# A two-layer decode step with finer pieces: K turned in halves or later, V of seven pairs in 2 KB pieces with one copy of P, new tables

## The chip, the cores and the metric

The kernel runs on one core of one Trainium2 chip. The metric is the device time of one execution in microseconds. The core's engines work beside each other and wait for one another on semaphores: TensorE (PE, with its weight loads shown as PEld), VectorE (DVE), ScalarE (ACT), GpSimd (POOL), and SyncE (SP), which here only issues transfers. Each engine takes its own instructions in the order in which they were written.

## The reference

Two layers, each an attention over a cache and a gated product, for 4 sequences with one new token each (bf16 in and out):

```python
# B=4, D=512, 32 query heads, 8 K/V heads, cache of 4096 keys, head size 128, F=1792
def _A_ref(x, k_cache, v_cache, wq, wo):
    q = (x @ wq) in heads;  k, v = caches, each head used by 4 query heads
    p = _softmax(einsum("bhqd,bhkd->bhqk", q, k) * (128 ** -0.5))
    return einsum("bhqk,bhkd->bhqd", p, v) in rows @ wo
def _B_ref(x, w_gate, w_up, w_down):
    return (_sigmoid(x @ w_gate) * (x @ w_up)) @ w_down

x = A_x
x = x + _A_ref(_layernorm(x), A_k_cache, A_v_cache, A_wq, A_wo)
x = x + _B_ref(_layernorm(x), B_w_gate, B_w_up, B_w_down)
x = x + _A_ref(_layernorm(x), A_k_cache, A_v_cache, A_wq, A_wo)   # same caches and weights
x = x + _B_ref(_layernorm(x), B_w_gate, B_w_up, B_w_down)
```

One K or one V of one K/V head and one sequence is 4096 x 128 in bf16, 1 MB. There are 64 of them, and both layers read all of them.

## The kernel before

**Pairs and steps.** The work is cut into 32 pairs: a layer, a sequence and two K/V heads, in the order of the table `ORDER`. The main loop (L1754) has 33 steps. Step k computes scores and softmax of pair k and the product with V (PV) of pair k-1; its parts stand in a fixed order with nine numbered places (0 to 8) between them, and tables say which further work stands at which place.

**Slots and loads.** K and V lie in 12 slots of 1 MB. 31 of the 64 tiles, named in `RET`, stay in SBUF from layer 1 to layer 2; the others are loaded twice. SP issues the loads in the order of the string `LOADS`, and `pump()` issues the next one as soon as a slot is free; a slot becomes free when the scores (`scores`, L1163) have read a K, or PV (L1365) a V. So the place of a score or PV group on PE sets when a load goes out. Loads have 8 KB per partition in one piece; the two V of the last pair come in four parts with 2 KB each (`v_parts`). The 4 MB of wq become four more slots when the last q product has read them, in step 27; the loads left then, 8 MB, are the last ones.

**One step of attention.** DVE turns K in place with a 32x32 stream transpose (`k_turn`, L1148), whole or as two halves. `first_turn` turns the first K of the next pair at one of three places, and the second K follows before place 4. The table `STEP` holds those choices and whether the first PV stands before the score products (`pv_first`). PE multiplies K with a spread q (L1163), DVE takes maxima (L1200 to L1206), PE spreads them over the partitions (L1223), DVE reduces again (L1236), ACT computes the exponential (L1248) with its sum, POOL adds sums (L1262), PE turns the result (`ptrans`, L1293) into the PSUM tile `PT`. From there 16 pieces of 32x64 are copied to `pT`, by ACT (L1319) and DVE (L1313); `SHARE` gives for each pair how many quarters DVE takes (0: all 16 on ACT, 1: 12 and 4, 2: 8 and 8). PV of one head is 32 matmuls in four groups, each waiting for its quarter of P; `PV_WIDE` repeats the four columns of P up to that width. After normalising (L1456) comes the product with wo (`wo_mm`, L1509, or in row form with a turn, L1487 to L1500, where `WO_ROW` says so), and `wo_add` (L1530) adds it to x. The last pair writes its exponential in the order in which the keys lie in the turned rows, with a stride of four, and its P is copied in two halves (L1300, L1301).

**The pass between the layers.** For each sequence, when its last pair of layer 1 is done, a pass of 23 parts runs: layer norm sums (L742 and L804), up and gate products (L963), gating, turning of the row (L1006), down product (L1077, L1099), layer norm, q product (L1024), its scaling and turning (L1038 to L1055), spreading of q (L868 to L893). `PLACES` gives each part's step and place. `FILL` adds matmuls with no use (L1182) at some places. After the last step come the output's layer norm and gated product (L1889 to L1945) and the store of 4x512 values.

## Time and profile before

| | us |
|---|---|
| median of 3 runs | 304.77 (304.65 to 306.59) |
| profiled execution, own time | 305.46 |
| its span, first to last instruction | 303.7 |
| mean granted clock of TensorE | 0.864 |
| PE / PEld busy | 227.6 / 158.5 |
| DVE / ACT / POOL busy | 206.3 / 130.7 / 26.2 |
| loads | 116.35 MB, mean 383 GB/s |

The profile is of one execution. Busy time of an engine is the time in which it carries out an instruction; waiting and issuing are not in it. A row of a group reads: line, engine, operation, written and read tiles, shapes, count, busy us and mean ns of one, and the engine's idle time just ahead of it with what ended that. A row of the timeline has the start in us from the span's start, the duration, and "x" with the number of instructions that were put together. The clock is a share of TensorE's full speed.

### The profile page before, as it was taken

What the parts mean: (1) busy time and instruction counts of PE and PEld (TensorE: products, weight loads), DVE (VectorE), ACT (ScalarE), POOL (GpSimd) and SP (SyncE); (2) the same over time, 40 slices, a digit from 0 to 9 for tenths busy, and PEclk for the clock granted to TensorE, in tenths of its full rate; (3) what the DMA queues carried; (4) which work ended last, traced back from release to release, by engine and by line L of the source; (5) the groups of instructions that cost most, each with busy time, mean ns of one, the idle gap of its engine ahead of it and who ended that gap; (6) DMA issues with size and microseconds to landing.
All of it is one profiled execution on the core that took longest, in us unless ns stands there. A gap on an engine that the chain in (4) does not pass through costs nothing.

```text
span 303.7 us, 11574 instructions
## 1 busy us (share of the span) xinstructions
PE 227.6 (75%) x5043; PEld 158.5 (52%) x5043; DVE 206.3 (68%) x611; ACT 130.7 (43%) x522; POOL 26.2 (9%) x108
## 2 busy tenths in 40 slices
PE   0355268589668888686996878788868988987896
PEld 0331024456544565465564656655445865665685
DVE  4727577877639359666952798884689467779834
ACT  1012074654505247344371676614566472547420
POOL 0000000000000010000000100000101100012200
PEclk9999999778857998996697777958875997999799
DMA  7999999999999989999999999999999998999910
GB/s 289 422 406 401 417 415 421 419 419 421 418 418 398 396 327 381 421 423 420 413 401 410 420 422 412 419 418 396 377 407 423 401 409 309 364 404 423 395 70 3
DMA packets 19166, 116.35 MB, mean 383 GB/s; under 512 B 1960, under 2 KB 1964, under 8 KB 6444
## 3 DMA queue, kind: packets, MB, share of 16 engines
q1 hardware_dynamic: 19116, 115.62, 94.0%
q8 instruction: 39, 0.64, 0.8%
q14 instruction: 11, 0.09, 0.1%
HBM read 115.61 MB, written 0.00 MB: 381 GB/s over the span
## 4 chain that ended last, share of the span: by engine, by line
PE 37%; DMA 35%; DVE 14%; SPq 6%; ACT 4%; issue 2%; POOL 0%; DVEq 0%
DMA slot<-in_A_v_cache_dram 24%; PE O_ps L1365 11%; PE S_ps L1163 7%; DMA wd<-in_B_w_down_dram 6%; DVE slot L1148 6%; DMA wo<-in_A_wo_dram 5%; PE M_ps L1024 3%; SPq L521 3%; ACT pT L1319 3%; PE O_ps L1509 3%; PE MS L1182 2%; SPq L540 2%; DVE pT L1313 1%; DVE small L1200 1%; PE M_ps L963 1%
## 5 line engine op out<-in xcount | busy, mean ns | idle before, releaser
L1319 ACT ACTIVATE pT<-PT 32x64 bf16<-32x64 f32 x396 | 84.9, 214 | 35.2 <-PE PT L1293 30.3
L1148 DVE STREAM_TRANSPOSE slot<-slot 128x1024 f32<-128x1024 f32 (+1 forms) x59 | 94.4, 1605 | 4.8 <-DMA slot<-in_A_k_cache_dram 4.7
L1365 PE MATMUL O_ps<-pT,slot 128*128 128x32 bf16 (+4 forms) x1952 | 66.9, 188 | 14.7 <-DMA slot<-in_A_v_cache_dram 8.5
L1365 PEld LDWEIGHTS O_ps<-pT,slot 128*128 128x128 bf16 x1952 | 60.8, 98 | 24.3 <-DMA slot<-in_A_v_cache_dram 9.4
L1163 PE MATMUL S_ps<-slot,qz 128*32 128x256 bf16 x976 | 47.7, 333 | 8.4 <-DVE slot L1148 5.0
L1248 ACT ACTIVATE pe<-S_ps,small 128x256 bf16<-128x256 f32 x32 | 15.5, 484 | 52.5 <-DVE small L1236 52.4
L1163 PEld LDWEIGHTS S_ps<-slot,qz 128*32 128x32 bf16 x976 | 25.6, 110 | 21.4 <-DVE slot L1148 6.9
L1262 POOL TENSOR_TENSOR small<-small 128x1 f32<-128x1 f32 x64 | 12.3, 193 | 221.2 <-ACT pe L1248 218.7
L1313 DVE CAST pT<-PT 32x64 bf16<-32x64 f32 x100 | 22.0, 220 | 3.7 <-PE PT L1293 2.2
L1509 PE MATMUL O_ps<-oT,wo 128*128 128x32 bf16 x640 | 21.3, 186 | 3.2 <-ACT wo L636 1.7
L636 ACT ACTIVATE wo<-M_ps 128x512 bf16<-128x512 f32 x14 | 8.3, 595 | 34.3 <-PE M_ps L626 34.2
L1509 PEld LDWEIGHTS O_ps<-oT,wo 128*128 128x128 bf16 x640 | 19.4, 99 | 4.9 <-DVE oT L1456 2.3
L626 PE MATMUL M_ps<-wo,row 64*128 64x512 bf16 x56 | 12.2, 524 | 8.0 <-DMA wo<-in_A_wo_dram 5.2
L1456 DVE TENSOR_TENSOR oT<-O_ps,rden 128x8 bf16<-128x8 f32 x31 | 5.0, 161 | 19.1 <-PE O_ps L1365 15.5
L641 DVE CAST wo<-M_ps 128x512 bf16<-128x512 f32 x14 | 9.5, 680 | 12.0 <-PE M_ps L626 11.8
L1200 DVE TENSOR_REDUCE small<-S_ps 128x1 f32<-128x256 f32 x32 | 13.2, 412 | 5.8 <-PE S_ps L1163 5.6
L1182 PE MATMUL MS<-ident_bf 128*128 128x256 bf16 x79 | 15.1, 332 | 2.4 <-DVE rden L1281 2.0
L893 POOL TENSOR_TENSOR qz<-qc,norm 128x128 bf16<-128x128 bf16 x32 | 12.6, 399 | 42.2 <-ACT qc L879 42.0
L1223 PE MATMUL MS<-row_max,mask_f 128*128 128x16 bf16 x64 | 6.7, 177 | 10.3 <-DVE row_max L1206 10.1
L1223 PEld LDWEIGHTS MS<-row_max,mask_f 128*128 128x128 bf16 x64 | 4.2, 105 | 17.5 <-DVE row_max L1206 14.8
L1293 PE MATMUL PT<-ident_bf,pe 128*128 128x128 bf16 x64 | 10.0, 244 | 3.7 <-ACT pe L1248 3.5
L1182 PEld LDWEIGHTS MS<-ident_bf 128*128 128x128 bf16 x79 | 7.8, 114 | 5.7 <-DVE rden L1281 2.2
(142 smaller groups left out, 230.6 us busy)
## 6 DMA issues: line engine op xcount, KB each, us to landing
slot<-in_A_v_cache_dram SPq DMA_DIRECT2D x51, 1024.0 KB, 9.9
slot<-in_A_k_cache_dram SPq DMA_DIRECT2D x40, 1024.0 KB, 10.0
wq<-in_A_wq_dram SPq DMA_DIRECT2D x4, 1024.0 KB, 7.6
wo<-in_A_wo_dram SPq DMA_DIRECT2D x8, 512.0 KB, 16.5
wq<-in_A_k_cache_dram SPq DMA_DIRECT2D x3, 1024.0 KB, 10.0
slot<-in_A_v_cache_dram SPq DMA_DIRECT2D x8, 256.0 KB, 16.6
wg<-in_B_w_gate_dram SPq DMA_DIRECT2D x2, 896.0 KB, 15.3
wu<-in_B_w_up_dram SPq DMA_DIRECT2D x2, 896.0 KB, 11.2
```

Source lines behind the costliest of these rows:

```text
L626: (lambda h, i, rows: lambda e: e.matmul(ps[h][:, :], lhsT=spread_w[i][rows, :], rhs=wo_sb[rows, c + i, :], start=(i == 0), stop=(i == 1), ...
L893: lambda e: e.tensor_tensor(qz_sb[z][:, :, 0:4 * REP].rearrange("p i (a r) -> p i a r", r=REP), qc_sb[:, b, u:u + 2, :, :].rearrange("p u ...
L1148: dve(lambda e: e.transpose(kf, kf), writes=[f"s{st}"])
L1163: (lambda t, b2, e_, w0, s: lambda e: e.matmul(S_ps[p][32 * s:32 * s + 8 * REP, 0:2 * P], lhsT=qzf[:, w0:w0 + 8 * REP], rhs=ktv[:, :, s, : ...
L1182: lambda e: e.matmul(MS[:, 2 * P:4 * P].rearrange("p (i m) -> p i m", i=2), lhsT=ident_bf[:, :], rhs=wide_id, start=True, stop=True,)
L1200: lambda e: e.tensor_reduce(m, S_ps[p][:, 0:2 * P], AX.X, ALU.max),
L1248: lambda e: e.activation(to, frm, ACTF.Exp, bias=nm_sb[p], scale=exp_scale, accum_out=sm_sb[p][0],),
L1262: (lambda n: lambda e: e.tensor_tensor(sm_sb[p][n + 1], sm_sb[p][n], top(sm_sb[p][n]), ALU.subtract))(n),
L1313: (lambda dst, frm: lambda e: e.tensor_copy(dst, frm))(dst, frm),
L1319: (lambda dst, frm: lambda e: e.activation(dst, frm, ACTF.Copy))(dst, frm),
L1365: (lambda x, c, j: lambda e: e.matmul(O_ps[p][:, ul * OW:ul * OW + PV_WIDE[g]].rearrange("p (w n) -> p w n", n=REP), lhsT=vv[:, x * JG + c ...
L1509: (lambda c, r: lambda e: e.matmul(wide_out(O_ps[p], OWO + c, nb), lhsT=wo_sb[:, u * REP + r, bass.ds(2 * P * (c // 2) + c % 2, P, step=2) ...
```

## The change

Eight things change.

1. The first K of a pair may be turned in halves, the second half one place later; the second K may be turned at one of three places (before place 4 as before, after place 5, or after place 7 at the end of the step). `STEP` holds both choices (`cut`, `late`).
2. Seven pairs get `SHARE` 6 (pairs 6, 12, 24, 27) or 7 (pairs 5, 19, 28). Their V are loaded in 2 KB pieces, in the order of four quarters of the keys (12 loads; the two V of pair 28 stay from pair 24), their exponential is read with a stride from PSUM and written plainly, and P is then one 128x256 copy, by ACT (6) or DVE (7). PV of a head is one group of 32 matmuls that waits for that copy.
3. The last exponential also reads with the stride and writes plainly.
4. With `WO_ROW` 2, the turn behind the row form of wo and the addition to x are put off to the next place or wo product (`undone`, `finish`).
5. `LAST` offers other orders for the last step; the table's value picks 0, the order of before.
6. `ORDER` and `RET` are new: sequence 3 of layer 2 ends with heads 2 and 3 rather than 6 and 7, and of that last pair only one V comes in four parts. 31 tiles are still kept.
7. `PLACES`, `FIRST_AT`, `LOADS`, `WO_AT`, `WO_ORDER`, `WO_TURN`, `WSUM`, `AHEAD` are new.
8. `SHARE`, `PV_WIDE` and `FILL` are new also for the other pairs: small copies of P on ACT from 396 to 320, on DVE from 100 to 64.

In the core of the diff, the tables are written in one line each, those of order and retention are left out:

```diff
-SHARE = (0, 1, 0, 2, 0, 1, 2, 0, 0, 2, 2, 1, 1, 1, 0, 0, 0, 0, 1, 1, 1, 0, 0, 2, 0, 1, 1, 2, 1, 1, 1)
+SHARE = (2, 2, 0, 0, 1, 7, 6, 0, 1, 1, 0, 0, 6, 2, 0, 0, 0, 0, 1, 7, 1, 0, 0, 1, 6, 1, 1, 6, 7, 0, 2)
-STEP = (6, 6, 6, 9, 5, 22, 12, 19, 6, 21, 16, 22, 9, 10, 23, 12, 9, 9, 9, 21, 21, 15, 19, 18, 21, 12, 15, 4, 3, 8, 0, 7, 8)
+STEP = (59, 9, 16, 35, 65, 37, 14, 24, 24, 9, 71, 6, 4, 59, 70, 12, 18, 30, 18, 40, 58, 9, 18, 12, 2, 11, 27, 10, 53, 25, 69, 48, 18)
-PV_WIDE = (32, 32, 32, 96, 32, 64, 48, 32, 48, 64, 32, 32, 48, 48, 32, 48, 32, 32, 32, 48, 64, 32, 32, 128, 48, 64, 48, 48, 64, 32, 96, 48)
+PV_WIDE = (32, 48, 64, 64, 32, 32, 32, 64, 48, 48, 32, 32, 48, 32, 96, 32, 64, 48, 64, 48, 32, 32, 64, 96, 64, 64, 48, 64, 96, 64, 64, 64)
-WO_ROW: 1 for pairs 7, 8, 14, 20, 27, 28, 31
+WO_ROW: 2 for pairs 7, 8, 12, 14, 15, 28; 1 for pairs 11, 19, 20, 22, 26, 27, 29
 PLACES, batch 3 (step counted from the batch's first, place in the step):
-        (1, 8), (1, 8), (1, 8), (1, 8), (2, 0), (2, 0),
-        (2, 1), (2, 1), (2, 2), (2, 2), (2, 4), (2, 6),
-        (2, 6), (2, 7), (2, 7), (2, 7), (2, 7), (2, 7),
-        (2, 7), (3, 0), (3, 0), (3, 4), (3, 6),
+        (1, 8), (2, 0), (2, 0), (2, 1), (2, 2), (2, 2),
+        (2, 2), (2, 2), (2, 2), (2, 3), (2, 3), (2, 6),
+        (2, 6), (2, 8), (2, 8), (2, 8), (2, 8), (2, 8),
+        (2, 8), (3, 0), (3, 0), (3, 2), (3, 2),
-FILL: 79 matmuls in 18 places
+FILL: 90 matmuls in 25 places
...
@@ -500,6 +502,13 @@
     def take():
         return free.pop(0)
 
+    def by_quarters(n):
+        return n < NU - 2 and SHARE[n // 2] > 5
+
+    for b in range(Bn):
+        for u in RET[b]["v"]:
+            assert by_quarters(pos[0, b, u]) == by_quarters(pos[1, b, u])
+
     def v_parts(s, n):
         _, b, u = seq[n]
         rows = A_v_cache[b, u].rearrange("(a p j) d -> a p (j d)", a=4, p=P)
@@ -535,6 +544,9 @@
                     continue
                 src = A_v_cache[b, u].rearrange("(p j) d -> p (j d)", p=P)
             dst = slot[s][:, :]
+            if kind == "v" and by_quarters(n):
+                dst = dst.rearrange("p (a m) -> p a m", a=4)
+                src = A_v_cache[b, u].rearrange("(a p j) d -> p a (j d)", a=4, p=P)
             S.dma(
                 "sp",
                 (lambda dst, src: lambda e: e.dma_start(dst, src))(dst, src),
@@ -1134,6 +1146,8 @@
             lambda: q_spread(b0, 1),
         ]
 
+    half_turned = set()
+
     def k_turn(i, part=None):
         if i >= NU or not loaded("k", i):
             return
@@ -1143,6 +1157,10 @@
         st = where["kt", b, u]
         kf = slot[st][:, :].bitcast(dt.float32)
         half = NJ * DH // 4
+        if part == 0:
+            half_turned.add(i)
+        else:
+            half_turned.discard(i)
         if part is not None:
             kf = kf[:, part * half:(part + 1) * half]
         dve(lambda e: e.transpose(kf, kf), writes=[f"s{st}"])
@@ -1151,6 +1169,7 @@
         l, b, _ = seq[2 * g]
         p = g % 2
         i = 2 * g + ul
+        assert i not in half_turned
         st = where["kt", b, seq[i][2]]
         ktv = slot[st].rearrange("p (x s j t k e) -> p x s j t k e", x=XJ, s=4, j=2, t=2, e=2)
         qzf = qz_sb[p].rearrange("p i w -> p (i w)")
@@ -1241,9 +1260,9 @@
             writes=["rmw", f"nm{p}"],
         )
         to, frm = pe_sb[p].rearrange("p j m -> p (j m)"), S_ps[p][:, 0:2 * P]
-        if g == NP - 1:
-            to = pe_sb[p].rearrange("p j (k x) -> p j x k", x=XJ)
-            frm = frm.rearrange("p (j x k) -> p j x k", j=2, x=XJ)
+        if g == NP - 1 or SHARE[g] > 5:
+            to = pe_sb[p].rearrange("p j (k x) -> p j k x", x=XJ)
+            frm = frm.rearrange("p (j x k) -> p j k x", j=2, x=XJ)
         act(
             lambda e: e.activation(
                 to,
@@ -1301,6 +1320,14 @@
             dve(lambda e: e.tensor_copy(pT_last[64:P, :], PT[64:P, 0:2 * P]), reads=["PT"], writes=["q1"])
             return
         pT = pT_sb[p]
+        if SHARE[g] > 5:
+            to = pT.rearrange("p x n j h -> p (x n j h)")
+            keys = [f"pT_{x}{a}" for x in range(XJ) for a in ("", "_0", "_1", "_2")]
+            if SHARE[g] == 6:
+                act(lambda e: e.activation(to, PT[:, 0:2 * P], ACTF.Copy), reads=["PT"], writes=keys)
+            else:
+                dve(lambda e: e.tensor_copy(to, PT[:, 0:2 * P]), reads=["PT"], writes=keys)
+            return
         src = PT[:, 0:256].rearrange("p (n a h) -> p n a h", n=16, h=REP)
         for x in range(XJ):
             for a in range(4):
@@ -1328,6 +1355,30 @@
         s = where["v", b, u]
         pT = pT_sb[p]
         vv = slot[s].rearrange("p (j d) -> p j d", d=DH)
+        if by_quarters(i):
+            assert PV_WIDE[g] >= 2
+            pq = pT.rearrange("p x n j h -> p (x n j h)").rearrange("p (j n a h) -> p j n a h", j=2, a=4, h=REP)
+            vq = slot[s].rearrange("p (a s j d) -> p a s j d", a=4, s=4, j=2)
+            fns = []
+            for a in range(4):
+                for sj in range(8):
+                    fns.append(
+                        (lambda a, c, j: lambda e: e.matmul(
+                            O_ps[p][:, ul * OW:ul * OW + PV_WIDE[g]].rearrange("p (w n) -> p w n", n=REP),
+                            lhsT=vq[:, a, c, j, :],
+                            rhs=pq[:, j, 4 * ul + c, a, :].unsqueeze(1).broadcast_to([P, PV_WIDE[g] // REP, REP]),
+                            start=(a == 0 and c == 0 and j == 0),
+                            stop=(a == 3 and c == 3 and j == 1),
+                        ))(a, sj // 2, sj % 2)
+                    )
+            rd = [f"s{s}"] + [f"pT_{x}{a}" for x in range(XJ) for a in ("", "_0", "_1", "_2")]
+            if ul == 0:
+                S.group("pe", fns, reads=rd, writes=[f"O{p}"])
+            else:
+                S.last_write[f"O{p}"] = S.group("pe", fns, reads=rd)
+            if l == 1 or not kept("v", i):
+                free.append(where.pop(("v", b, u)))
+            return
         if PV_WIDE[g] < 2:
             many = 2 - PV_WIDE[g]
             for x in range(XJ):
@@ -1494,14 +1545,22 @@
                     )
             S.group("pe", fns, reads=rd, writes=[f"O{p}"])
             act(lambda e: e.activation(row_f, rows, ACTF.Copy), reads=[f"O{p}"], writes=["row0"])
-            fns = []
+            turns = []
             for i in range(2):
-                fns.append(
+                turns.append(
                     (lambda i: lambda e: e.matmul(
                         turned[:, :, i, 0:nb], lhsT=row_f[:, i:2 * P:2], rhs=sel_f[:, :, 0:nb], start=True, stop=True
                     ))(i)
                 )
-            S.group("pe", fns, reads=["row0", "sel"], writes=[f"O{p}"])
+
+            def turn():
+                S.group("pe", turns, reads=["row0", "sel"], writes=[f"O{p}"])
+                wo_add(g, p)
+
+            if WO_ROW[g] == 2:
+                undone.append(turn)
+            else:
+                turn()
             return
         for c in range(KD):
             for r in range(2 * REP):
@@ -1532,9 +1591,16 @@
             writes=[f"x{b0}", f"x{b1}"],
         )
 
+    undone = []
+
+    def finish():
+        while undone:
+            undone.pop()()
+
     def wo_pair(g, p):
         wo_mm(g, p)
-        wo_add(g, p)
+        if not WO_ROW[g]:
+            wo_add(g, p)
 
     ln_a(0, Bn)
     ln_b(Bn)
@@ -1599,6 +1665,7 @@
     assert max(WSUM) < (NP - 3, 8)
 
     def do_steps(g, w):
+        finish()
         if FILL.get((g, w)):
             fill(FILL[g, w])
         for m in wo_steps.pop((g, w), ()):
@@ -1672,6 +1739,7 @@
         )
 
     assert NP % 2 == 0
+    LAST = (0, 1, 2, 4, 5, 6)[STEP[NP] % 6]
     XS, XM = S_ps[0], M_ps[0][:, 0:1]
 
     def x_others():
@@ -1741,6 +1809,7 @@
 
     def do_wo(gs, p):
         for g in gs:
+            finish()
             waiting.remove(g)
             wo_pair(g, p)
 
@@ -1784,11 +1853,20 @@
         if nxt is not None and fresh.get(seq[2 * nxt][:2]) != k:
             q_blocks(nxt)
         do_steps(k, 0)
-        turn_at, pv_first, halves = STEP[k] % 3, STEP[k] // 3 % 2, STEP[k] // 6
+        turn_at, pv_first, cut, late = STEP[k] % 3, STEP[k] // 3 % 2, STEP[k] // 6 % 4, STEP[k] // 24
+        halves = cut % 2 == 1 and sg is not None and nxt is not None
 
         def first_turn(at):
             if nxt is not None and turn_at == at:
-                k_turn(2 * nxt)
+                k_turn(2 * nxt, 0 if cut > 1 else None)
+                pump()
+            elif nxt is not None and cut > 1 and turn_at + 1 == at:
+                k_turn(2 * nxt, 1)
+                pump()
+
+        def second_turn(at):
+            if nxt is not None and late == at:
+                k_turn(2 * nxt + 1, 1 if halves else None)
                 pump()
 
         first_turn(0)
@@ -1804,7 +1882,6 @@
                     do_wo(wo_ready(k + 1)[:1], (k + 1) % 2)
 
         wo_at(0)
-        halves = halves and sg is not None and nxt is not None
         if pv_first and vg is not None and sg is not None:
             pv(2 * vg)
             pump()
@@ -1820,16 +1897,16 @@
         wo_at(1)
         first_turn(2)
         do_steps(k, 3)
-        if nxt is not None:
-            k_turn(2 * nxt + 1, 1 if halves else None)
-            pump()
+        first_turn(3)
+        second_turn(0)
         do_steps(k, 4)
         if vg is not None and not pv_first and sg is not None:
             pv(2 * vg)
             pump()
         wo_at(2)
         do_steps(k, 5)
-        if sg == NP - 1:
+        second_turn(1)
+        if sg == NP - 1 and LAST & 3 == 0:
             ptrans(sg)
         if vg is not None:
             if sg is not None:
@@ -1837,15 +1914,25 @@
                 pump()
                 normalise(vg)
                 normed[seq[2 * vg]] = k
+                if sg == NP - 1 and LAST & 3 == 1:
+                    ptrans(sg)
             else:
+                if LAST & 3 == 2:
+                    ptrans(vg)
+                if LAST & 4:
+                    do_wo([g for g in wo_ready(k) if g != vg], (vg + 1) % 2)
+                    finish()
+                    x_others()
                 pv_last(vg, 0, 0, 4)
                 normalise_last(0)
                 waiting.remove(vg)
                 assert len(waiting) <= 1
-                do_wo(wo_ready(k), (vg + 1) % 2)
+                if not LAST & 4:
+                    do_wo(wo_ready(k), (vg + 1) % 2)
+                    finish()
+                    x_others()
                 assert not waiting
                 others_done()
-                x_others()
                 mean_old()
                 pv_last(vg, 1, 0, 2)
                 mean_old_mm()
@@ -1862,6 +1949,7 @@
             ptrans(sg)
         wo_at(3)
         do_steps(k, 7)
+        second_turn(2)
         if vg is not None and sg is not None and vg in ends:
             close(vg, k)
         if k == NP - 3:
```

## The prediction

> **What bounds the kernel now.** I read the page first (busy shares, slices, queues, chain), then a table of 4 us windows, then the groups by shape, and last the timeline of three places that the windows point to.

> ```profile
> span 303.7 us, 11574 instructions
> PE 227.6 (75%) x5043; PEld 158.5 (52%) x5043; DVE 206.3 (68%) x611; ACT 130.7 (43%) x522; POOL 26.2 (9%) x108
> q1 hardware_dynamic: 19116, 115.62, 94.0%
> PE 37%; DMA 35%; DVE 14%; SPq 6%; ACT 4%; issue 2%; POOL 0%; DVEq 0%
> ```

> The load queue is busy for 94.0% of the span, more than any engine, yet the chain that ends last is only 35% transfers: no resource is full all the time. Where the stream breaks is in the windows (columns: PE, PEld, DVE, ACT, POOL busy us, granted clock, DMA share, GB/s).

> ```profile
> core 0: us, PE busy (x) PEld busy (x) DVE busy (x) ACT busy (x) POOL busy (x), PEclk, DMA share, GB/s
> 104.00:108.00 4.00, 3.02 (x64) 1.68 (x64) 1.71 (x7) 0.69 (x1) 0.00 (x0) 1.00 1.03 367
> 108.00:112.00 4.00, 3.83 (x109) 3.09 (x109) 3.03 (x16) 2.61 (x12) 0.76 (x2) 1.00 0.75 268
> 112.00:116.00 4.00, 3.34 (x100) 2.40 (x88) 2.01 (x3) 2.32 (x11) 0.74 (x3) 1.00 1.00 373
> 216.00:220.00 4.00, 2.95 (x86) 2.19 (x86) 3.31 (x7) 2.76 (x13) 0.76 (x2) 1.00 0.94 350
> 244.00:248.00 4.00, 3.02 (x97) 2.44 (x94) 3.25 (x9) 2.75 (x11) 0.74 (x3) 1.00 1.02 420
> 252.00:256.00 4.00, 4.00 (x67) 1.90 (x59) 3.72 (x9) 0.71 (x2) 0.00 (x0) 0.59 0.69 233
> 256.00:260.00 4.00, 3.64 (x101) 2.78 (x94) 2.91 (x7) 1.24 (x4) 0.16 (x1) 1.00 0.99 391
> 260.00:264.00 4.00, 3.67 (x77) 2.81 (x77) 2.90 (x16) 2.31 (x12) 0.23 (x2) 1.00 0.98 344
> 264.00:268.00 4.00, 3.22 (x97) 2.21 (x86) 2.33 (x12) 1.12 (x4) 0.00 (x0) 1.00 0.93 363
> 284.00:288.00 4.00, 3.74 (x98) 2.58 (x95) 3.21 (x10) 1.88 (x9) 1.99 (x8) 0.75 1.04 385
> ```

> The undisturbed rate is 420 GB/s; 115.62 MB at that rate take 275 us. The three windows from 104 fall short of it by 53, 152 and 47 GB/s, together 252 x 4 us / 420 = 2.4 us of lost transfer; 252 to 268 loses 3.3 us in the same way, 216:220 another 0.7. Behind the last window shown the stream ends, and what follows is a tail of computing. Gains can come from these places and from the tail. Elsewhere the stream runs, and shorter work only waits for it.

> **Row copies of P (seven pairs).** Each pair copies P to the PV matmuls' layout in 16 pieces.

> ```profile
> L1319 ACT ACTIVATE pT<-PT 32x64 bf16<-32x64 f32 x396 | 84.9, 214 | 35.2 <-PE PT L1293 30.3
> L1313 DVE CAST pT<-PT 32x64 bf16<-32x64 f32 x100 | 22.0, 220 | 3.7 <-PE PT L1293 2.2
> L1248 ACT ACTIVATE pe<-S_ps,small 128x256 bf16<-128x256 f32 x32 | 15.5, 484 | 52.5 <-DVE small L1236 52.4
> L879 ACT ACTIVATE qc<-M_ps 128x128 bf16<-128x128 f32 x8 | 1.9, 280 | 9.2 <-PE M_ps L868 9.1
> L1898 ACT ACTIVATE slot<-PT 128x128 f32<-128x128 f32 x1 | 0.3, 278 | 6.6 <-PE PT L1889 6.6
> DMA slot<-in_A_v_cache_dram 24%; PE O_ps L1365 11%; PE S_ps L1163 7%; DMA wd<-in_B_w_down_dram 6%; DVE slot L1148 6%; DMA wo<-in_A_wo_dram 5%; PE M_ps L1024 3%; SPq L521 3%; ACT pT L1319 3%; PE O_ps L1509 3%; PE MS L1182 2%; SPq L540 2%; DVE pT L1313 1%; DVE small L1200 1%; PE M_ps L963 1%
> ```

> The tables take the pieces from 396 to 320 on ACT and from 100 to 64 on DVE: 76 x 0.214 + 36 x 0.220 = 24.2 us. Seven whole 128x256 copies come instead. No row has that copy; it lies between 0.280 (L879, half as many columns) and 0.484 us (as many, with the exponential), and I take 0.45, near the second, so 3.2 us. Net 21.0 of 106.9 us, 19.6%. The chain holds 3% + 1% of 303.7 us of these copies, 12.1 us, of which some 4.5 lie in the tail (the 2.73 quoted there and eight DVE pieces), costed below: 7.6 x 0.196 = **-1.5 us**. Bounds: 0, if the stream was the next limit wherever they stood, and -3.0, if it was nowhere and pairs on the chain were hit twice as often. PV now waits for all of P and not for its first quarter, but all is there in 0.45 us, where the first ACT quarter took 4 x 0.214.

> The exponential of these pairs reads PSUM with a stride. For the kind, L879 (strided read, 280 ns) against L1898 (plain, 278 ns) says that it costs nothing; bound 7 x 0.36 us = +2.5, were it as dear as the strided write of the last exponential (0.83 us below, against (15.5 - 0.83) / 31 = 0.47 for the others).

> **V in 2 KB pieces.** Twelve loads change from 8 KB to 2 KB pieces and one V less comes as separate quarters. The rows for 2 KB are the last V's quarters: 385 GB/s at a share of 1.04 in 284:288, against 420. That is 1.05 MB at 2.72 for 2.50 us, +0.2 each, 12 x 0.2 - 0.2 = +2.2 us if each stands on a full stream. Some fall beside the gaps of steps 6 and 26, and stretches of the chain are not transfers at all (65%): I take **+0.8**, between 0 and +2.2. [...]

> **Step 26, the deepest gap.** Here the order of batch 3's pass and of the loads is told by the timeline.

> ```profile
> 243.69 0.33 SPq L540 DMA_DIRECT2D slot<-in_A_v_cache_dram  x1
> 245.43 0.33 SPq L540 DMA_DIRECT2D slot<-in_A_k_cache_dram  x1
> 249.99 0.39 PE L742 MATMUL M_ps<-xT,small 128*128 128x4 f32 x2
> 251.75 0.81 PE L963 MATMUL M_ps<-wu,xc_bf 128*1 128x448 bf16 x8 [0.26 <-DVE norm L815]
> 252.33 1.07 PE L1163 MATMUL S_ps<-slot,qz 128*32 128x256 bf16 x16
> 253.44 11.88 SPq L540 DMA_DIRECT2D slot<-in_A_v_cache_dram  x5
> 256.12 1.14 PE L1365 MATMUL O_ps<-pT,slot 128*128 128x64 bf16 x32
> 265.69 0.80 SPq L540 DMA_DIRECT2D wq<-in_A_k_cache_dram  x2
> ...
> slot<-in_A_v_cache_dram SPq DMA_DIRECT2D x51, 1024.0 KB, 9.9
> ```

> From 245.43 to 253.44 no load is issued: the next V waits for a slot that only the scores at 252.33 free, and those stand on PE behind the layer norm (L742, L804) and the first wu product. Queued data runs out and 252:256 moves 233 GB/s. The new places put these scores straight behind L742, so they can run at 250.4 and the V goes out at about 251.4, 2.0 us sooner. The first PV of that step, at 256.12 before, moves ahead of the second wu half and of wg with four fills; it frees its V about 2 us sooner, but sets the gate path back by 1.14 + some 0.6 less the 1.07 of the scores that left: +0.7. That PV also waits for the V issued at 243.69; by the median of 9.9 us to landing (last row, from the page) it is there at 253.6, where PE would now arrive at 252.6 or so: up to 1.0 more, with wu, wg and pair 27's scores queued behind it. At the end of that path the q product releases wq (265.69), and 8 MB of loads wait for it. So between -2.2 (the gap's 3.3 us mostly filled) and +1.7; I take **-0.9**, as the V that starts sooner is certain from the order on PE and the landing is not.

> **Step 20.** 216:220 is short because a K waits there for a PV that stands behind two q row products.

> ```profile
> 212.55 2.03 PE L1024 MATMUL M_ps<-wq,xc_bf 128*1 128x512 bf16 x16
> 214.63 0.96 PE L1365 MATMUL O_ps<-pT,slot 128*128 128x48 bf16 x32
> 215.62 0.33 SPq L540 DMA_DIRECT2D slot<-in_A_k_cache_dram  x1
> ```

> The PV now precedes the last product (half of 2.03): the K goes 1.0 us sooner, against 0.7 us of loss: **-0.5** (0 to -0.7). The like edit in step 6 puts the first PV ahead of a q half but adds four fills there; both are about a microsecond: 0 (-0.9 to +0.5).

> **Tail.** The last pair's scores end with the stream, and from then on each step follows the one before.

> ```profile
> 286.00 2.73 ACT L1319 ACTIVATE pT<-PT 32x64 bf16<-32x64 f32 x12 [2.27 <-PE PT L1293]
> 288.24 0.08 DVE L1236 DVE_READ_ACCUMULATOR2_ANT small<- 128x1 f32 x1
> 288.76 0.83 ACT L1248 ACTIVATE pe<-S_ps,small 128x256 bf16<-128x256 f32 x1
> 289.77 1.55 PE L1365 MATMUL O_ps<-pT,slot 128*128 128x96 bf16 x32
> ```

> The exponential's maximum is there at 288.32, but ACT is in the twelve copies of pair 30 until 288.73: with eight (DVE takes the other four, off this path) it starts 0.4 sooner. Its write is now contiguous, 0.83 to 0.47: -0.36. PV of pair 30 goes from 96 to 64 columns wide; the 64-wide one above takes 1.14, so -0.4 for the one that stands between the exponential and the last pair's PV. Sum **-1.2** (-1.9 with both PVs; 0 if the last K, now turned in halves about the softmax of pair 30, comes later by as much).

> **Edits at nothing.**

> ```profile
> L1182 PE MATMUL MS<-ident_bf 128*128 128x256 bf16 x79 | 15.1, 332 | 2.4 <-DVE rden L1281 2.0
> L1148 DVE STREAM_TRANSPOSE slot<-slot 128x1024 f32<-128x1024 f32 x38 | 46.4, 1220 | 2.6 <-DMA slot<-in_A_k_cache_dram 2.5
> ```

> 38 to 42 half turns and whole turns 21 to 20, 11 more fills, wider PVs up to 96 columns, put-off row turns and `wo` row forms: DVE (68%) and PE have the room while transfers run; without that cover the fills would be 11 x 15.1 / 79 = +2.1 us, the four half turns less one whole (two halves), 2 x 1.22 = +2.4. Retained K and V change places only; the megabytes stay.

> **Sum.** -1.5 + 0.8 - 0.9 - 0.5 - 1.2 = **-3.3 us**. The profiled execution took 305.46 us (span 303.7 and 1.76 around it) and would come to 302.2; the median of the runs is 0.69 lower, 304.77, and comes to **301.5**. A measurement of this kernel can tell some 1% from no change: 301.7 to 307.8 is "the same".

> **Rivals.** *Gaps close (298.7).* With the copies' relief at -3.0 and step 26 at -2.2, the rest as above: -6.1. For: two loads of step 26 move by 2 us, into a gap of 3.3, and pairs 6, 24 and 27 beside the gaps are among the seven. Against: a load goes out only when its own slot is free, so a gap closed in one step can open in the next.

> *Nothing upstream arrives (305.3).* The stream keeps its length, 2 KB costs its +2.2 (or the strided read its +2.5), and only the tail's -1.2 and step 20's -0.5 remain: +0.5 (+0.8). For: 94.0% queue share. That the change does not do what it says is this case too: copies that were hidden anyway.

> *K turned too late (308.3).* In eight steps the second K is now turned behind the copies and the step's last small products, right ahead of the next step.

> ```profile
>   DVE slot L1148: 11.9, 11
> ```

> That row (PE's idle time ahead of scores, us and times, by what ended it) says that 11 turns already keep PE waiting 11.9 us, 1.08 each. PE takes its work in order, so PV, `wo` and the pass behind those scores wait, and with them every slot that they free. Eight more such waits are 8.6 us; the chain's share outside transfers and their queue is 55%, so +4.7, less the tail's 1.2: +3.5. It decides from the point where a late turn ends after PE's other work of the next step's first half. Against: in most steps the first K's scores and a PV (about 1 us each) stand ahead of the second K's.

> **How the numbers follow.** Forecast 0.36 (own range 299.8 to 303.3), gaps close 0.24, nothing arrives 0.20, late turns 0.20. Faster by over 1%: 0.24 and somewhat over half of the forecast's, less what the gap case leaves above 301.7: 0.44. Slower by over 1%: 0.20 and a little of the third case, 0.22. Within 1%: 0.34. The range, 297.5 to 308.5, takes in the gap case and most of the late turns.

> **What would show it.** Right: the 252:256 window above 330 GB/s and the V of step 26 issued within 7 us of the load before; wq's K within 264 to 266 or sooner; last exponential 0.47 us; whole copies 0.38 to 0.48; windows with 2 KB pieces near 385 to 400 GB/s. Wrong: PE's idle time on K turns well over 11.9 us, whole copies near 0.8, or a gap of the stream that has only moved to another step.

## Result and profile after: 1.1% slower, and the profiled loss lies behind the release of wq

The changed kernel took 310.3 us (median; 307.8 to 311.1), 1.0114 times the kernel before beside it, with a 95% interval of 1.0066 to 1.0161. Run once more as a control on another chip it took 1.0057 (1.0012 to 1.0102). The forecast was 1.1% faster. Ratios compare undisturbed runs of both kernels (the profile of `block_shifted` is of a disturbed one, so no time is read from it), and only ratios of one chip are held against each other closely, since the kernel before itself had medians of 305.7 to 307.4 us over the chips.

The page of the changed kernel, with the lines that answer to those of before:

```profile
span 309.1 us, 11450 instructions
PE 227.0 (73%) x5030; PEld 160.6 (52%) x5030; DVE 201.2 (65%) x581; ACT 116.7 (38%) x452; POOL 26.2 (8%) x108
q1 hardware_dynamic: 23292, 115.62, 92.9%
PE 37%; DMA 30%; DVE 17%; SPq 8%; ACT 4%; issue 3%; POOL 0%; DVEq 0%; ACTq 0%
```

ACT is 14 us less busy and DVE 5 us, near the 21.0 us in all that the copies' arithmetic gave, and transfers hold less of the chain (30% for 35%). The span is 5.4 us longer. The windows show where these are not lost (columns as before):

```profile
96.00:100.00 4.00, 3.28 (x65) 2.32 (x65) 1.99 (x8) 0.37 (x1) 0.00 (x0) 1.00 1.05 387
108.00:112.00 4.00, 2.32 (x65) 1.53 (x66) 1.23 (x7) 0.66 (x2) 0.76 (x2) 0.94 0.93 337
216.00:220.00 4.00, 2.77 (x83) 2.27 (x81) 2.56 (x9) 0.07 (x1) 0.00 (x0) 0.83 1.02 424
252.00:256.00 4.00, 3.83 (x82) 2.21 (x78) 3.77 (x9) 1.15 (x2) 0.00 (x0) 1.00 0.94 348
260.00:264.00 4.00, 3.45 (x35) 1.40 (x39) 2.68 (x15) 3.09 (x13) 0.00 (x0) 0.72 0.97 356
264.00:268.00 4.00, 3.79 (x103) 2.72 (x95) 1.68 (x6) 0.18 (x1) 0.00 (x0) 0.86 0.49 151
288.00:292.00 4.00, 4.00 (x85) 2.88 (x88) 2.77 (x14) 2.27 (x10) 2.18 (x8) 0.63 0.49 182
```

The gaps that the prediction named have shrunk: 268 to 337 GB/s at 108, 350 to 424 at 216, 233 to 348 at 252. Summed over all 4 us windows, the stream leads before's by 0.78 MB at 264 us, 1.86 us at 420 GB/s. In the window behind it falls to 151 GB/s (363 before) and the whole lead is gone. From there both streams run alike and end in the same window (182 and 176 GB/s at 288). The 5.4 us come after that point, on PE; in the chain that ended last, no transfer stands behind 262 us, neither before nor after the change:

```profile
265.75 1.70 SPq L552 DMA_DIRECT2D wq<-in_A_k_cache_dram  x3
...
270.77 0.89 PE L1366 MATMUL O_ps<-pT,slot 128*128 128x64 bf16 x25
273.11 0.38 PE L1366 MATMUL O_ps<-pT,slot 128*128 128x64 bf16 x7 [1.45 <-issue]
279.04 4.35 PE L1366 MATMUL O_ps<-pT,slot 128*128 128x96 bf16 x64
283.54 3.64 ACT L1346 ACTIVATE pT<-PT 32x64 bf16<-32x64 f32 x16 [2.11 <-PE PT L1312]
294.12 0.47 ACT L1267 ACTIVATE pe<-S_ps,small 128x256 bf16<-128x256 f32 x1 [1.07 <-DVE small L1255]
294.86 1.12 PE L1416 MATMUL O_ps<-pT,slot 128*128 128x64 bf16 x32
```

wq is released at 265.75 us, as before (265.69). The last exponential starts at 294.12 (288.76 before), and what follows takes 15 us in both, of which more below. Between the maxima of pairs 28 and 29 pass 6.8 us (3.7 before), of pairs 30 and 31 6.9 (5.2), and 2.5 us (1.8) to the last exponential. In these rows stand a stop of PE of 1.45 us in the middle of one PV with nothing named that it waits for, a PV of pair 28 of 4.35 us for 64 matmuls, and sixteen copies of pair 29.

### The profile page after: what moved, and what is told of

Its sections match the earlier page's. It is cut to its first block, busy times and chain, and to the rows that moved or that the text cites. A ratio compares the mean times of both kernels' runs of the same rounds, so it can differ in the third digit from the quotient of the medians.

```text
span 309.1 us, 11450 instructions
## 1 busy us (share of the span) xinstructions
PE 227.0 (73%) x5030; PEld 160.6 (52%) x5030; DVE 201.2 (65%) x581; ACT 116.7 (38%) x452; POOL 26.2 (8%) x108
## 3 DMA queue, kind: packets, MB, share of 16 engines
q1 hardware_dynamic: 23292, 115.62, 92.9%
## 4 chain that ended last, share of the span: by engine, by line
PE 37%; DMA 30%; DVE 17%; SPq 8%; ACT 4%; issue 3%; POOL 0%; DVEq 0%; ACTq 0%
DMA slot<-in_A_v_cache_dram 16%; DMA slot<-in_A_k_cache_dram 8%; DVE slot L1166 8%; PE O_ps L1416 7%; DMA wo<-in_A_wo_dram 6%; PE S_ps L1182 5%; PE O_ps L1366 5%; SPq L552 5%; ACT pT L1346 3%; SPq L530 2%; PE M_ps L1036 2%; PE O_ps L1568 2%; PE M_ps L975 2%; PE MS L1201 2%; DVE pT L1340 1%
## 5 line engine op out<-in xcount | busy, mean ns | idle before, releaser
L1166 DVE STREAM_TRANSPOSE slot<-slot 128x1024 f32<-128x1024 f32 (+1 forms) x62 | 96.8, 1568 | 3.5 <-DMA slot<-in_A_k_cache_dram 3.4
L1346 ACT ACTIVATE pT<-PT 32x64 bf16<-32x64 f32 x320 | 68.6, 214 | 30.6 <-PE PT L1312 26.5
L1416 PE MATMUL O_ps<-pT,slot 128*128 128x32 bf16 (+3 forms) x1504 | 52.3, 189 | 11.2 <-DMA slot<-in_A_v_cache_dram 8.4
L1416 PEld LDWEIGHTS O_ps<-pT,slot 128*128 128x128 bf16 x1504 | 47.8, 99 | 17.6 <-DMA slot<-in_A_v_cache_dram 9.4
L1182 PE MATMUL S_ps<-slot,qz 128*32 128x256 bf16 x976 | 47.0, 329 | 13.1 <-DVE slot L1166 11.2
L1267 ACT ACTIVATE pe<-S_ps,small 128x256 bf16<-128x256 f32 x32 | 15.1, 473 | 77.2 <-DVE small L1255 77.0
L1182 PEld LDWEIGHTS S_ps<-slot,qz 128*32 128x32 bf16 x976 | 24.7, 108 | 26.6 <-DVE slot L1166 15.6
L1281 POOL TENSOR_TENSOR small<-small 128x1 f32<-128x1 f32 x64 | 12.3, 193 | 208.4 <-ACT pe L1267 205.9
L1568 PE MATMUL O_ps<-oT,wo 128*128 128x32 bf16 x576 | 19.5, 187 | 1.1 <-DVE oT L1507 0.6
L1568 PEld LDWEIGHTS O_ps<-oT,wo 128*128 128x128 bf16 x576 | 18.0, 101 | 2.9 <-DVE oT L1507 1.5
L1366 PE MATMUL O_ps<-pT,slot 128*128 128x32 bf16 (+3 forms) x448 | 17.0, 197 | 2.3 <-issue 1.4
L1366 PEld LDWEIGHTS O_ps<-pT,slot 128*128 128x128 bf16 x448 | 16.1, 104 | 4.3 <-issue 2.9
L1201 PE MATMUL MS<-ident_bf 128*128 128x256 bf16 x90 | 15.8, 299 | 2.1 <-DVE rden L1300 1.6
L1340 DVE CAST pT<-PT 32x64 bf16<-32x64 f32 x64 | 14.1, 220 | 1.6 <-PE PT L1312 0.6
## 6 DMA issues: line engine op xcount, KB each, us to landing
slot<-in_A_v_cache_dram SPq DMA_DIRECT2D x51, 1024.0 KB, 11.8
slot<-in_A_k_cache_dram SPq DMA_DIRECT2D x41, 1024.0 KB, 11.4
wq<-in_A_wq_dram SPq DMA_DIRECT2D x4, 1024.0 KB, 7.7
wq<-in_A_k_cache_dram SPq DMA_DIRECT2D x3, 1024.0 KB, 10.5
wg<-in_B_w_gate_dram SPq DMA_DIRECT2D x2, 896.0 KB, 15.1
wu<-in_B_w_up_dram SPq DMA_DIRECT2D x2, 896.0 KB, 15.5
wd<-in_B_w_down_dram SPq DMA_DIRECT2D x1, 1024.0 KB, 17.0
```

The source lines that it names most:

```text
L1166: dve(lambda e: e.transpose(kf, kf), writes=[f"s{st}"])
L1182: (lambda t, b2, e_, w0, s: lambda e: e.matmul(S_ps[p][32 * s:32 * s + 8 * REP, 0:2 * P], lhsT=qzf[:, w0:w0 + 8 * REP], rhs=ktv[:, :, s, : ...
L1201: lambda e: e.matmul(MS[:, 2 * P:4 * P].rearrange("p (i m) -> p i m", i=2), lhsT=ident_bf[:, :], rhs=wide_id, start=True, stop=True,)
L1267: lambda e: e.activation(to, frm, ACTF.Exp, bias=nm_sb[p], scale=exp_scale, accum_out=sm_sb[p][0],),
L1340: (lambda dst, frm: lambda e: e.tensor_copy(dst, frm))(dst, frm),
L1346: (lambda dst, frm: lambda e: e.activation(dst, frm, ACTF.Copy))(dst, frm),
```

## Experiments

All are the changed kernel with a few table entries altered, unless said otherwise. "Release to exponential" is, in the profiled execution, from the first load into wq to the last exponential: 23.1 us before, 28.4 changed.

**Parts undone.** `tail_as_before` takes `STEP`, `SHARE`, `PV_WIDE`, `WO_ROW`, `WO_AT` of the last pairs from before; `no_late_turns` and `no_quarter_pairs` undo one idea throughout:

```diff
-STEP: late 1 or 2 in 17 steps
+STEP: late 0 everywhere                      # no_late_turns
-SHARE 6 or 7 in seven pairs
+SHARE 0 to 2, V in 8 KB pieces               # no_quarter_pairs
```

> The changed kernel with the entries of before for the last four steps alone: turning (STEP 28 to 31), copies of P of pairs 29 and 30, PV widths, wo form and place of pairs 28 to 31. Tail theory (the load stream ends at the same time in both kernels, about 290 us, and the 5.4 us were lost on PE's chain through steps 28 to 31): 305 to 306.5 us, last exponential near 289 to 290 us of the span. Late-turn theory (the second K turned late somewhere in the 31 steps): 309 to 310.5. Pieces theory (2 KB pieces and whole copies): 309 to 310.5.

> The changed kernel with every second K turned before place 4, as before the change. Late-turn theory: PE's waits for turned K fall from 26.8 us towards 12 and the time to 306 or less. Tail theory: 309.5 to 310.5, waits nearly as they were, since on DVE few instructions change places. Pieces theory: the same as the tail theory.

> The changed kernel with the seven pairs back at 8 KB pieces and 16 copies of P (shares 0 to 2). Pieces theory: 306 to 307.5. Tail theory: 309.5 to 311, the stream's gap at 264 to 268 us smaller or elsewhere, its end at 290 as before. Late-turn theory: no difference, 310.

Measured: 1.0138 (1.0057 to 1.0220) for the tail, 1.0268 (1.0178 to 1.0358) without late turns, 1.0396 (1.0297 to 1.0494) without the seven pairs. The first cannot be told from the change itself, and the other two are slower than it: taking parts out of tables that were made with them says little of what each part costs. The tail with before's entries lost the wide PV and the sixteen copies and found other waits. Its timeline:

```profile
283.01 0.64 PE L1182 MATMUL S_ps<-wq,qz 128*32 128x256 bf16 x16 [1.15 <-DVE wq L1166]
285.09 2.31 DVE L1166 STREAM_TRANSPOSE wq<-wq 128x2048 f32<-128x2048 f32 x1
287.41 0.42 DVE L1219 TENSOR_REDUCE small<-S_ps 128x1 f32<-128x256 f32 x1
```

Here scores wait for a K turn, and pair 30's maximum waits on DVE behind the next K's whole turn (2.31 us): the copies' place on the chain is taken by DVE, so that theory failed in the form in which it was put. For the late turns the row of the scores' waits decides (us and times). The changed kernel:

```profile
  DVE slot L1166: 26.8, 26
```

Without late turns:

```profile
  DVE slot L1166: 21.1, 24
```

PE's waits for turned K have grown from 11.9 us (11 times) to 26.8 (26 times). Without the late places 5.7 of these 14.9 us go, and the kernel is slower all the same. What made the others is open.

**Parts alone, on the tables of before.** `code_alone` has the new code with all old tables; `quarters_on_before` adds the seven pairs there; `before_tail_copies` gives one copy to pairs 28 to 30 (and 22, 24, which keep V for them).

> The changed code with all tables of before: on the engines only the last exponential differs (strided read, plain write). By the prediction's term: 0.36 us less than before, the last exponential 0.47 us; all theories agree. If the strided read costs as the strided write did: no difference.

> All tables of before, and only the part of the seven pairs: the same seven pairs of heads get 2 KB pieces of V and one copy of P. By the prediction's terms (copies -1.5, pieces +0.8): 0.7 us less than the code alone, so equal to it within the noise. Pieces theory (2 KB costs its full 2.2 us of stream): 2 us more. If the copies' relief reaches the end as where the new tables lose it (9 us more without): 3 us or more less.

> All tables of before, one copy of P (and 2 KB pieces) only for the pairs 28, 29 and 30 of the end and the pairs 22 and 24 whose kept V they use. By the prediction's working of the tail (ACT's copies delay the last exponential by 0.4 us, its write 0.36): 0.8 us less than before, ratio 0.995 to 0.999. If the late copies are covered by PE's chain as in the changed kernel: 1.000 to 1.004.

Measured: 1.0063 (1.0016 to 1.0110), 1.0030 (0.9994 to 1.0067), 1.0031 (0.9995 to 1.0066). The last exponential is 0.47 us in each, and none is ahead of before. The code alone even lies above 1, by as much as the control of the whole change, though on the engines only its last exponential differs; `quarters_on_before`, with the same code, came to 1.0030 on another chip. Whether the new code itself costs something is therefore open. On the tables of before, the seven pairs neither cost nor bring anything that these intervals show.

**The stop.** `block_shifted` adds two filling matmuls at the end of each of steps 8 to 23; `early_shift` puts 32 and `early36` 36 in steps 1 to 4. `light` stands for two entries:

```diff
+FILL: (k, 8): 2 more for k = 8 to 23         # block_shifted
+FILL: eight times 4 in steps 1 to 4          # early_shift; 5 and 4 in turn: early36
-SHARE[29] 0, PV_WIDE[28] 96
+SHARE[29] 1, PV_WIDE[28] 64                  # light
```

> The changed kernel with two more filling matmuls at the end of each of steps 8 to 23 (32 in all), which moves every later 16 KB block of PE's program by 32 matmuls. In the three kernels so far that kept the seven pairs, PE stands still for 1.5 to 2.1 us seven matmuls ahead of the end of pair 27's first PV with nothing to wait for, and the clock then falls to half. Program theory (the stop is the fetch of the next block of PE's program, late behind the queued loads): the stop is elsewhere or shorter, no half-clock stretch of 6.8 us at 275, pair 29's maximum near 275 us instead of 277.6, 306.5 to 308.5 us in all. Data theory (it is that PV's own data or its slot): the stop stays in that PV, time as before the shift or above, 310 to 312.

> The changed kernel with two entries altered: pair 29's copies of P 12 on ACT and 4 on DVE (16 on ACT), pair 28's PV 64 wide (96). Tail theory in its narrow form (these two lie on PE's chain of steps 29 and 30: 4.35 us of PV at half clock, 3.64 us of copies): 308 to 309. If other work takes their place: 310 to 311.

> Both edits together. If stop and chain add up: 305 to 307; the last exponential at 289 to 291 us of the span (294.1 in the changed kernel, 288.8 before). If the tail goes on being late for another reason: 309 to 311.

> The changed kernel with 32 filling matmuls in steps 1 to 4, four at a time, where PE waits for weights and turned K anyway. It moves the program's blocks as the fills in steps 8 to 23 did, but adds nothing ahead of the last q product. Program theory: no stop in pair 27's first PV, wq released near 265.7 as without, the last exponential 23 to 24 us behind it (28.4 in the changed kernel, 23.1 before): 305.5 to 307.5 us, ratio 0.997 to 1.004. If the earlier fills had helped for another reason (clock in steps 8 to 23): the stop or another loss comes back, 309 to 311.

> The same with pair 29's copies 12 and 4 and pair 28's PV 64 wide. If these entries still lie on the chain once the stop is gone: 1 to 2 us less than the shift alone. If both only showed up through the half clock behind the stop: the same as the shift alone.

> The changed kernel with 36 filling matmuls in steps 1 to 4. PE then enters the block in question about as close to the release of wq as in the kernel with fills in steps 8 to 23, where its next block was fetched 0.9 to 1.4 us after the entry (3.4 us in the changed kernel). If the fetch waits behind queued loads: no stop between 268 and 275 us, pair 29's maximum 4.3 us behind pair 28's (6.8 in the changed kernel). If the stop makes the difference at the end: 1.5 to 3 us less than the changed kernel beside it. If not: the same time as the changed kernel, with another wait in its place.

> The same with pair 29's copies 12 and 4 and pair 28's PV 64 wide. If stop and these entries are the whole loss behind the release of wq: last exponential 23 to 24 us behind it (28.4 changed, 23.1 before), time within 1 us of before. If the stream before it is later too: above that.

| kernel | ratio (95%) | PE's stop, us | half clock behind the release, us | release to exponential, us |
|---|---|---|---|---|
| block_shifted | 1.0036 (1.0005 to 1.0068) | none near | (not compared) | (not compared) |
| light_pairs | 1.0073 (1.0036 to 1.0110) | 1.81 | 0 | 25.7 |
| shifted_light | 1.0086 (1.0036 to 1.0136) | none near | 0 | 23.7 |
| early_shift | 1.0110 (1.0069 to 1.0152) | 1.52 | 0 | 24.8 |
| early_light | 1.0101 (1.0067 to 1.0135) | 1.86 | 3.4 | 27.2 |
| early36 | 1.0063 (1.0026 to 1.0099) | none near | 0 | 23.2 |
| early36_light | 1.0108 (1.0068 to 1.0148) | 2.12 | 3.4 | 27.4 |

The fourth column is the time between the release and the last exponential in which PE's granted clock stood at half. In the profiles the two columns before the last go with the last one: 23.2 and 23.7 us without the stop, 24.8 and 25.7 with it, 27.2 and 27.4 with it and 3.4 us of half clock. The ratios do not follow that order.

With 32 matmuls put in early, the stop moves by 32 matmuls, out of the PV into the scores ahead of it. The timeline of `early_light`:

```profile
269.90 0.98 PE L1182 MATMUL S_ps<-slot,qz 128*32 128x256 bf16 x26
272.75 0.61 PE L1182 MATMUL S_ps<-slot,qz 128*32 128x256 bf16 x6 [1.86 <-issue]
```

So it belongs to the program's position, not to that PV's data. I counted PE's records (matmuls, weight loads and its sequencer's own) up to the first instruction behind each stop of over 0.2 us with nothing named: in 54 of 67, over all the kernels here, the count is 193 modulo 256. The other 13 are a stop of 0.3 us ahead of the last pair's first PV, which starts 0.1 us behind DVE's half of the copy of P that it reads. Each of the 54 is preceded by one 16 KB packet on the instruction queue that ended 1.2 to 1.6 us earlier. The changed kernel's trace has 39 such packets (0.64 MB in its page) for PE's 10132 records, and of the 39 stretches of 256 records that begin at a count of 193 (the last one shorter) each has one of them. So I read them as PE's program, in blocks of 256 records; the rows do not say what a packet holds. In the changed kernel PE enters the block ahead of the stop, 256 records earlier, at 267.29 us, and the next block's packet moves only at 270.7; in `early36` it enters at 267.54 and the packet moves at once. The rows of the DMA queues (packets, MB, share) of the changed kernel, for 267.3 to 270.5 us and then for 270.5 to 271.8:

```profile
q1 hardware_dynamic: 455, 1.22, 99.9%
...
q1 hardware_dynamic: 74, 0.54, 101.0%
q8 instruction: 1, 0.02, 4.6%
```

The same of `early36` for 267.5 to 269.0 us:

```profile
q1 hardware_dynamic: 148, 0.30, 92.5%
q8 instruction: 1, 0.02, 5.9%
```

The difference that these rows show is the load queue: in `early36` the block is entered 0.5 us behind the release of wq, when the stream is still down (161 GB/s at 264 to 268); in the changed kernel 1.5 us behind it, with three loads of 1 MB newly issued. The 128 matmuls of that block take PE 4.4 us there (267.29 to 271.66); the next block's packet ends at 271.6, and PE goes on at 273.11. In `early36_light`, entered 0.5 us behind the release as well, but with a stream at 269 GB/s in that window, the packet moved 4.1 us later and the stop was back. In `shifted_light`, without the stop, it moved 0.9 us behind the entry. Before has no such stop there: its packet moves 3.0 us behind the entry, and PE, waiting 1.4 us for other engines on the way, needs 5.5 us for these 256 records. Of the changed kernel's packets, the 36 that move while loads run do so 0.8 to 5.4 us behind the entry (median 3.0), the three after the loads' end 0.3 to 1.0. That queued loads hold a packet back is my reading of these profiles: no row shows what it waits for. The stop was up to 2.1 us long.

In `early36` the PV runs through, and the release-to-exponential time is that of before, 23.2 for 23.1 us:

```profile
272.10 1.09 PE L1366 MATMUL O_ps<-pT,slot 128*128 128x64 bf16 x32
```

Its median is nevertheless that of the control (below). In its profile the release of wq came at 267.05, 1.3 us later than the changed kernel's, so what it saved behind the release it had paid ahead of it. Up to 104 us, well behind its 36 fills, its stream has moved as much as the control's; by 116 us it is 0.53 MB behind, 1.3 us at 420 GB/s. What holds it up there is open.

**The same program twice.**

> The changed kernel once more, as the control on this chip: 1.011 of before, 1.007 to 1.016; the stop in pair 27's first PV, seven matmuls ahead of its end.

The control's ratio is at the lower end of what was expected, and its profile differs from the first one of the same program. Windows of the first:

```profile
276.00:280.00 4.00, 3.22 (x46) 2.40 (x44) 2.89 (x6) 0.00 (x0) 0.00 (x0) 0.50 1.01 420
280.00:284.00 4.00, 4.00 (x77) 3.86 (x78) 3.63 (x7) 1.01 (x5) 1.09 (x5) 0.72 1.01 424
```

Of the control, and the row of pair 28's PV in its timeline:

```profile
276.00:280.00 4.00, 3.20 (x78) 2.75 (x74) 3.46 (x6) 0.00 (x0) 0.26 (x1) 1.00 1.01 420
280.00:284.00 4.00, 3.21 (x85) 2.28 (x82) 4.00 (x8) 3.16 (x15) 1.10 (x5) 1.00 1.02 422
```

```profile
278.20 2.88 PE L1366 MATMUL O_ps<-pT,slot 128*128 128x96 bf16 x64
```

Both had the stop (1.45 and 1.55 us). In the first the clock fell to half behind it and pair 28's PV took 4.35 us; in the control it stayed full and the PV took 2.88. Release to exponential is 24.7 us there, the span 305.6. Between release and exponential the first had 10.2 us of half clock (275.4 to 282.2 and 289.0 to 292.4), the control none. So of the 5.4 us of the first profile, 3.5 differ between two executions of one program, and 1.9 stay. Stops of 1.45 and 1.55 us were thus followed by 6.8 us of half clock in one execution and by none in the other.

Before's 23.1 us hold 3.4 us of half clock too (282.6 to 286.0; the window 284:288, shown in the prediction, stands at 0.75):

```profile
280.00:284.00 4.00, 2.29 (x64) 1.91 (x53) 3.67 (x9) 1.92 (x8) 0.19 (x1) 0.83 1.00 416
```

`code_alone`, with before's tables and no half clock there, takes 22.6. So at full clock the changed tables are 0.6 us longer here even without the stop (23.2 in `early36`), as far as one profile of each tells.

**The release of wq moved.** `early_light_26` is `early_light` with the first PV of step 26 put behind the softmax again. `q_first` and `q_first_light`, and `before_q_first` on the kernel before, put the last q product first:

```diff
 PLACES, batch 3, 20th part
-(3, 0)
+(2, 8)
```

> As the kernel with shift and both entries, and in step 26 the first PV (pair 25) is put behind the softmax again, so that the second half of wu and wg stand on PE ahead of it. If the load stream's lead (1.8 us at 264 us in the changed kernel) is lost because the q product that releases wq comes no sooner: wq is released about 1 us sooner and the time falls by as much. If the clock in the q product decides (20 matmuls took 2.5 us at half clock), no sooner: same time or longer, since that PV's slot is free later.

> The changed kernel, but the last eight q matmuls stand directly behind the other 24, ahead of pair 27's second scores (1.07 us and three small matmuls). Release theory (the loads behind wq set the end): wq released near 264.6 instead of 265.8, 1 us less than the changed kernel, ratio 1.002 to 1.006. Tail theory (PE's chain of the last four pairs sets it): the last exponential lies more than 24 us behind the release, time as the changed kernel, 1.006 to 1.011.

> The same with pair 29's copies 12 and 4 and pair 28's PV 64 wide. Release theory: as the run beside it. Tail theory: 1 to 2 us less than it, if the copies and the width are what is left on that chain; if neither, the same time as the changed kernel.

> The kernel of before with the same move. Release theory: wq released near 264.8 instead of 265.7, 0.7 us less than before, ratio 0.995 to 0.999; that would be the version ahead of both. Tail theory: no difference, 0.998 to 1.003.

`early_light_26` (1.0082; 1.0045 to 1.0119) released wq at 265.3 for 266.0, and the release-to-exponential time grew to 27.4 us. `q_first` came to 1.0060 (1.0021 to 1.0099), `q_first_light` to 1.0120 (1.0068 to 1.0173), before with the move to 1.0029 (0.9991 to 1.0066). In `q_first` the first load into wq goes out 1.1 us sooner than in the changed kernel, and the last exponential starts where the control has it (290.62):

```profile
264.67 0.38 SPq L552 DMA_DIRECT2D wq<-in_A_v_cache_dram  x1
290.71 0.47 ACT L1267 ACTIVATE pe<-S_ps,small 128x256 bf16<-128x256 f32 x1 [1.14 <-DVE small L1255]
```

The earlier release is taken back. The move changes the order of PE's work ahead of the stop and not its amount, and the stop was 1.94 us for the control's 1.55. As in the changed kernel, no transfer stands in the chain that ended last behind 262 us in the control and in `q_first`: there PE's chain through the last four pairs, with the copies on ACT, sets the end, and the stream's lead is worth nothing to it. That does not hold for every table. In `quarters_on_before` and `before_tail_copies` that chain runs through one V load of 16.5 us issued behind the release. None of the kernels here is ahead of before.

## Why the prediction was wrong

**The step that failed is the sum.** It added gains of the load stream (-1.5, -0.9, -0.5, +0.8) to the time at the end as if nothing stood between. As a sum they came about in the stream: 1.86 us of lead at 264 us, against the 2.1 that these terms make. Which term brought which part the windows do not separate, so that the figures agree so well may be luck. The release of wq, which the prediction itself named as what 8 MB of loads wait for, stayed at 265.7, and the lead went in the next window.

The gain of step 26 did reach the work ahead of the release. The q product starts 1.35 us sooner than before, but before runs it and the scores behind it at full clock:

```profile
262.78 1.71 PE L1024 MATMUL M_ps<-wq,xc_bf 128*1 128x512 bf16 x24
264.31 0.64 PE L1163 MATMUL S_ps<-slot,qz 128*32 128x256 bf16 x16
```

The changed kernel runs both in a stretch of half clock (the window 260:264 stands at 0.72, before at 1.00):

```profile
261.43 2.72 PE L1036 MATMUL M_ps<-wq,xc_bf 128*1 128x512 bf16 x24
263.92 1.07 PE L1182 MATMUL S_ps<-slot,qz 128*32 128x256 bf16 x16
```

These two rows are 1.44 us longer, and the 1.35 are gone. In `light_pairs`, with the same tables up to there, the product took 1.71 us and wq was released at 264.64. The prediction's sum had no clock in it. Nor would the release have counted: `q_first` and `light_pairs`, which release wq 1.1 us sooner, start the last exponential at 290.71 and 290.29 us, the control at 290.62; their stops, 0.4 and 0.3 us longer, are a part of that.

**The tail's term began too late.** Its pieces came as written: write 0.47 us, PV of 1.12 instead of 1.55. But from the last maximum to the end the profile has 15.4 us before (from 288.24) and 15.1 after (from 294.00), so 0.4 of the 1.2 us arrived. The last pair's first PV waits for DVE's half of the copy of P, and that copy starts 1.85 and 1.84 us behind the maximum, since DVE first runs the layer norm's instructions (288.36 to 290.07 before, 294.12 to 295.82 after). Before, where the wide PV covered it:

```profile
290.09 0.43 DVE L1301 CAST slot<-PT 64x256 bf16<-64x256 f32 x1
291.24 0.96 PE L1392 MATMUL O_ps<-slot,slot 128*128 128x48 bf16 x32
```

After, with the last pair's `PV_WIDE` at 64 for 48, which the prediction put at nothing:

```profile
294.00 0.08 DVE L1255 DVE_READ_ACCUMULATOR2_ANT small<- 128x1 f32 x1
295.84 0.43 DVE L1320 CAST slot<-PT 64x256 bf16<-64x256 f32 x1
296.37 1.09 PE L1443 MATMUL O_ps<-slot,slot 128*128 128x64 bf16 x32 [0.33 <-issue]
```

Above all, the tail was taken to begin with the last pair. It begins with the release of wq, and in the four steps behind it the change loses 5.3 us in the first profile and 1.6 in the control (28.4 and 24.7 for 23.1). Of these, the stop is 1.5 us; `early36` and `shifted_light`, without it, have 23.2 and 23.7. The half clock, 10.2 us of it against 3.4 before, goes with most of the rest of the first profile: the control, without it, has 3.7 us less.

**Terms that held.** Whole copies:

```profile
L1327 ACT ACTIVATE pT<-PT 128x256 bf16<-128x256 f32 x4 | 1.5, 383 | 4.1 <-PE PT L1312 4.1
L1329 DVE CAST pT<-PT 128x256 bf16<-128x256 f32 x3 | 1.2, 413 | 0.0
L1267 ACT ACTIVATE pe<-S_ps,small 128x256 bf16<-128x256 f32 x32 | 15.1, 473 | 77.2 <-DVE small L1255 77.0
```

0.38 and 0.41 us for an estimate of 0.45; the strided read cost nothing here (473 ns over all 32; the eight strided ones took 467 to 475). Where 2 KB pieces flow at a full queue the rate is 387 GB/s (96:100 above), near the 385 of the row for the last V. Step 26's V went out at 250.84 for an estimate of 251.4. Step 20's gap closed.

**The rivals.** The slower one (308.3 us, K turned too late) was nearest to the measured time, and the waits that it spoke of did grow to 26.8 us. But most of that growth was not the late places, and no such wait lies behind the release of wq in the first profile. Of the signs of being wrong that the prediction named, two came: these waits, and a gap of the stream that has only moved (151 GB/s at 264:268). "Nothing upstream arrives" had the right mechanism for the stream and the wrong size, since it left the tail's gain standing.

**What stays open.** Stop and half clock explain the profiles, each of one execution, but not the medians: the three kernels without the stop have ratios of 1.0036, 1.0063 and 1.0086, and the control, with it, 1.0057. How much of the 0.6 to 1.1% they make over many executions is therefore not settled. Nor is what brings the half clock, how much the new code alone costs, or why K turns keep PE waiting longer.

## What to carry to other kernels

Before adding gains of separate stages, follow each to the next point where everything waits for one event (here the release of wq), and ask whether that event comes sooner; if not, the gain ends there. Cost a tail from the last such event, not from the last piece of data, list what every engine still has to do in it, and test it by moving that event. Look at two executions of the same program before explaining a difference of one per cent: the two here were 3.5 us apart, one with 10.2 us of half clock where the other had none.
